# An FFT token mixer with a channel-mix behind it: the first transforms of later batches due 0.3 of a period sooner

## The chip, the cores and the metric

The kernel runs on one core of one Trainium2 chip. The metric is the device time of one execution in microseconds (us). Before the change the median was 607.15 us (three runs, 604.29 to 610.09).

TensorE (PE) multiplies, ScalarE (ACT) and VectorE (DVE) move results out of its accumulation banks and do the elementwise work, GpSimd (POOL) issues the loads of x, and SyncE (SP) issues nearly all other DMAs, one after the other in program order.

## The reference, cut to what matters

```python
# x: (8, 3072, 256) float32
X = np.fft.rfft(x, axis=1)
Yr = Xr @ w_r - Xi @ w_i + b_r
Yi = Xr @ w_i + Xi @ w_r + b_i
Y  = shrink(Yr, 0.01) + 1j * shrink(Yi, 0.01)     # sign(v) * max(|v| - 0.01, 0)
y  = np.fft.irfft(Y, n=3072, axis=1)              # tokens of the second half
xk = mu_k * y + (1 - mu_k) * y_prev;  xr = mu_r * y + (1 - mu_r) * y_prev
out = sigmoid(xr @ w_r2) * (relu(xk @ w_k) ** 2 @ w_v)
```

Each of the 8 batches passes through two transforms in two steps each (3072 = 96 x 32), and then through six token tiles of the channel-mix, which is the bulk of the matrix work.

## The kernel before

The transform of a batch of length 3072 is done as 96 x 32. Between the two steps of each transform the data change their layout by a "bounce": they are stored to device memory and read back differently. The stages of one batch are:

- `first`: first step of the forward transform (L279), 8 pairs of matmuls; results A are stored (L290, four stores of 384 KB), and when all four have landed they are read back as A2 (L304, eight reads of 192 KB). Each A store also sets off a load of x for the next batch (L68, from GpSimd).
- `middle`: second step, mixing with w_r and w_i, shrinking, first step back (L394, L422, L448); results V are stored in six groups of four 64 KB stores (L461) and read back (L472, four pieces of 384 KB): the second bounce.
- `last`: last step (L525), eight units; then the six token tiles (L611, L638, L655).

Below, "the boundary of batch b" (or boundary b) is the place where the last V stores of batch b, its read of V and its first L525 units stand.

```python
# in first(b): after the eviction of a group of A
def store(k):
    nc.sync.dma_start(out=Adr[b][:, 8 * q:8 * q + 8, :], in_=a)          # L290
    ...
        load_x(n // 4, n % 4)                                            # L68, next batch
    if q == 3:
        at(k + WRITE_US, fetch)
def fetch(k):
    for hf in range(2):
        A2[b, hf] = a2_pool.tile([128, NG // 2, D], BF16, name="A2")
        for cj in range(4):
            r0 = 24 * cj + 12 * hf
            nc.sync.dma_start(out=A2[b, hf][32 * cj:32 * cj + 32],       # L304
                              in_=Adr[b][r0:r0 + 12].rearrange("g n d -> n g d"))
...
# in middle(b): after the eviction of a group of V
def store(k):
    for cj in range(4):
        nc.sync.dma_start(out=Vdr[b][24 * cj + 4 * u:24 * cj + 4 * u + 4]...,
                          in_=vt[32 * cj:32 * cj + 32])                  # L461
    if u == NU - 1:
        at(k + (3.0 if b == 0 else WRITE_US), fetch)
def fetch(k):
    ...
    for q in (2, 3, 0, 1):
        nc.sync.dma_start(out=V2[b, q], in_=Vdr[b][:, 8 * q:8 * q + 8, :])   # L472
...
# order of the last step: the first unit needs pieces 2 and 3, the second pieces 0 and 1
order = ((1, 3), (0, 3), (0, 0), (0, 1), (0, 2), (1, 0), (1, 1), (1, 2))
```

A small planner in the kernel decides, while the program is built, in which order these units are put out. Each unit has a due time and a list of what it needs; among the units that its own clock calls ready, the one with the earliest due time is next. Engines execute in that fixed order. So a due time is not a time on the chip: it moves instructions, and with them the DMAs that hang on them, to another place in each engine's program.

```python
P = 71.5          # the planner's period, one batch
...
else:
    fb += first(b, s - 0.9 * P, s - 0.2 * P)
    fa += middle(b, s, s + 0.5 * P)
    fc += last(b, s + 0.75 * P, s + 0.95 * P)
```

## Time and profile before

| | before |
|---|---|
| median time | 607.15 us |
| span of the profiled run | 604.4 us |
| TensorE busy / VectorE / ScalarE | 94% / 86% / 72% |
| mean granted TensorE clock | 0.993 |
| waits of L525 for the read of V (PE and weight loads) | 12.8 us in 14 waits |

How to read this: TensorE is full, so its order is the time axis, and what costs time is only what makes it wait. The page's slices, the stretches of one period, TensorE's own timeline and the chain are shown in the prediction. The point to take from them is that in steady state nearly every period has 1 us of idle TensorE, and one has 4.

SyncE's own timeline around that place, at the boundary of batch 3 (start, duration of the issues together, operation, tensors, count):

```profile
241.86 1.88 SPq L461 DMA_DIRECT2D Vdr<-V  x4
244.44 0.68 SPq L290 DMA_DIRECT2D Adr<-A  x1
250.91 2.00 SPq L472 DMA_DIRECT2D V<-Vdr  x4
```

The read of V follows the last V stores with one A store between them. The reads of A come later, at 262.74.

### The profile page before, as it was taken

The numbers are of one execution on the slowest core, as the hardware profiler recorded it, in microseconds if no ns is written. First come the engines' busy times: TensorE is split into PE (matmuls) and PEld (weight loads), VectorE is DVE, ScalarE is ACT, GpSimd is POOL, SyncE is SP. The second block draws the span as 40 slices with busy tenths as digits, with TensorE's granted clock in tenths as the row PEclk, the third lists the DMA queues.
The fourth block names the chain that finished last, engine by engine and source line by source line (L and its number), as shares of the span: only waits on it lengthen the run. The fifth ranks groups of instructions, "written<-read, shape, count | busy, mean of one in ns | idle before, by whom it ended". The sixth has DMA issues, their size and how long they took to land.

```text
span 604.4 us, 12322 instructions
## 1 busy us (share of the span) xinstructions
PE 570.7 (94%) x4823; PEld 430.9 (71%) x4891; DVE 517.6 (86%) x839; ACT 436.3 (72%) x477; POOL 23.9 (4%) x53
## 2 busy tenths in 40 slices
PE   4977999999999999889999999999999999999996
PEld 3856766677767787667776777677776778776775
DVE  7677998789998899958988888979988889989983
ACT  6956986767776777567786768777787777667553
POOL 7001000000000000000000000000000000000000
PEclk9999999999999999989999999999999999999999
DMA  8945849864589555793569935785347834362224
GB/s 149 158 87 129 171 96 240 190 129 106 107 202 213 142 123 119 173 222 99 124 133 225 203 77 117 159 247 125 94 104 186 185 96 89 80 183 50 65 64 102
DMA packets 68878, 84.06 MB, mean 139 GB/s; under 512 B 9042, under 2 KB 53844, under 8 KB 68820
## 3 DMA queue, kind: packets, MB, share of 16 engines
q1 hardware_dynamic: 62916, 68.98, 45.8%
q0 software_dynamic: 5712, 14.03, 14.9%
q8 instruction: 38, 0.62, 0.4%
q10 hardware_dynamic: 192, 0.26, 0.2%
q14 instruction: 20, 0.16, 0.1%
HBM read 50.07 MB, written 47.19 MB: 161 GB/s over the span
## 4 chain that ended last, share of the span: by engine, by line
PE 80%; DMA 7%; DVE 5%; ACT 5%; issue 2%; SPq 1%; POOL 0%; ACTq 0%; POOLq 0%; DVEq 0%
PE banks L655 25%; PE banks L611 24%; PE banks L422 12%; PE banks L638 6%; DMA V<-Vdr 4%; PE banks L448 3%; PE banks L394 3%; PE banks L279 3%; PE banks L525 3%; ACT rl L617 2%; DMA Vdr<-V 2%; DMA xs<-in_x_dram 1%; ACT YT L226 1%; PE banks L352 1%; DVE Y L438 1%
## 5 line engine op out<-in xcount | busy, mean ns | idle before, releaser
L617 ACT ACTIVATE rl<-banks 128x1024 bf16<-128x1024 f32 x192 | 195.5, 1033 | 76.2 <-PE banks L611 75.2
L611 PE MATMUL banks<-xk,wk 128*128 128x512 bf16 x700 | 190.6, 379 | 5.3 <-ACT A L226 0.8
L655 PE MATMUL banks<-wv,k 128*128 128x256 bf16 x1536 | 183.4, 272 | 0.3 <-DVE k L623 0.3
L655 PEld LDWEIGHTS <-k 128*128 128x128 bf16 x1536 | 149.7, 98 | 30.3 <-issue 1.2
L623 DVE TENSOR_TENSOR k<-rl 128x1024 bf16<-128x1024 bf16 x192 | 131.1, 686 | 17.9 <-ACT rl L617 17.2
L611 PEld LDWEIGHTS <-wk 128*128 128x128 bf16 x768 | 73.0, 98 | 59.7 <-issue 3.5
L422 PEld LDWEIGHTS <-XT 128*128 128x128 bf16 x768 | 74.1, 98 | 17.2 <-issue 1.2
L422 PE MATMUL banks<-wr,XT 128*128 128x256 bf16 x384 | 73.3, 272 | 0.5 <-ACT YT L226 0.2
L422 PE MATMUL banks<-wi,XT 128*128 128x256 bf16 x384 | 73.3, 273 | 0.4 <-DVE XT L404 0.4
L589 DVE SCALAR_TENSOR_TENSOR xk<-diff,muk,YT 128x512 bf16<-128x512 bf16 x96 | 70.0, 745 | 0.5
L589 DVE SCALAR_TENSOR_TENSOR xr<-diff,mur,YT 128x512 bf16<-128x512 bf16 x96 | 68.9, 745 | 0.0
L666 DVE TENSOR_TENSOR o<-banks,rg 128x1024 f32<-128x1024 f32 (+1 forms) x49 | 58.7, 1197 | 5.8 <-PE banks L655 5.8
L226 ACT ACTIVATE YT<-banks 128x768 bf16<-128x768 f32 x60 | 46.4, 815 | 21.7 <-PE banks L525 19.0
L226 ACT ACTIVATE XT<-banks 128x1024 bf16<-128x1024 f32 (+2 forms) x46 | 44.9, 982 | 14.5 <-PE banks L394 14.3
L226 ACT ACTIVATE z<-banks 128x1024 bf16<-128x1024 f32 x38 | 38.9, 1024 | 22.0 <-PE banks L422 21.9
L638 PE MATMUL banks<-wrm,xr 128*128 128x256 bf16 x384 | 50.2, 274 | 1.7 <-ACT rl L617 1.5
L226 ACT ACTIVATE A<-banks 96x1024 bf16<-96x1024 f32 (+1 forms) x44 | 44.6, 1015 | 8.8 <-PE banks L279 6.7
L643 ACT ACTIVATE rg<-banks 128x1024 bf16<-128x1024 f32 x48 | 49.5, 1032 | 0.5 <-PE banks L638 0.5
L638 PEld LDWEIGHTS <-xr 128*128 128x128 bf16 x384 | 37.3, 98 | 12.4 <-issue 2.3
L226 ACT ACTIVATE V<-banks 128x1024 bf16<-128x1024 f32 x35 | 36.0, 1029 | 13.8 <-PE banks L448 9.8
L436 DVE TENSOR_TENSOR z<-z,bias 128x1024 bf16<-128x1024 bf16 x48 | 32.9, 686 | 9.5 <-ACT z L226 9.4
L525 PEld LDWEIGHTS <-V 96*128 96x128 bf16 x512 | 27.2, 98 | 13.5 <-DMA V<-Vdr 7.3
(100 smaller groups left out, 448.9 us busy)
## 6 DMA issues: line engine op xcount, KB each, us to landing
out_dram<-o SPq DMA_DIRECT2D x188, 128.0 KB, 2.3
xs<-in_x_dram POOLq DMA_DIRECT2D x32, 384.0 KB, 5.8
Vdr<-V SPq DMA_DIRECT2D x192, 64.0 KB, 1.8
V<-Vdr SPq DMA_DIRECT2D x32, 384.0 KB, 6.6
Adr<-A SPq DMA_DIRECT2D x24, 384.0 KB, 5.3
A<-Adr SPq DMA_DIRECT2D x48, 192.0 KB, 5.6
wk<-in_moe_w_k_dram POOLq DMA_DIRECT2D x1, 512.0 KB, 12.5
wv<-in_moe_w_v_dram POOLq DMA_DIRECT2D x1, 512.0 KB, 13.8
```

Source lines behind the costliest of these rows:

```text
L226: nc.scalar.activation(out, in_, AF.Copy, bias=0.0, scale=1.0)
L422: nc.tensor.matmul(o, lhs, w[:, c, :], start=(w is wr and c == 0), stop=(w is wi and c == NCD - 1))
L436: nc.vector.tensor_tensor(out=z, in0=z, in1=bias0 if u == 0 else bias, op=ALU.add)
L525: nc.tensor.matmul(pv[:, c, :, i, :], V2[b, n2 // 8][:, n2 % 8, 128 * c:128 * c + 128], FI, start=True, stop=True)
L589: nc.vector.scalar_tensor_tensor(out=m[:, c, :], in0=df[:, c, :], scalar=mu[:, c:c + 1], in1=yp[:, c, :], op0=ALU.mult, op1=ALU.add)
L611: nc.tensor.matmul(ps[:, 512 * f:512 * f + 512], wk[:, c, 128 * ff:128 * ff + 128], xk[:, c, :], start=(c == 0), stop=(c == NCD - 1))
L617: nc.scalar.activation(rl, ps, AF.Relu, bias=0.0, scale=1.0)
L623: nc.vector.tensor_tensor(out=k2, in0=rl, in1=rl, op=ALU.mult)
L638: nc.tensor.matmul(ps[:, 256 * q:256 * q + 256], xr[:, c, 128 * q:128 * q + 128], wrm[:, c, :], start=(c == 0), stop=(c == NCD - 1))
L643: nc.scalar.activation(rg, ps, AF.Sigmoid, bias=0.0, scale=1.0)
L655: nc.tensor.matmul(ps[:, 256 * q:256 * q + 256], K2[t][:, ff, 128 * q:128 * q + 128], wv[:, ff, :], start=(ff == 0), stop=(ff == NCF - 1))
L666: nc.vector.tensor_tensor(out=o[:, lo:hi], in0=ps[:, lo:hi], in1=rg[:, lo:hi], op=ALU.mult)
```

## The change

The intent, in the words that came with it: the first transforms of later batches are due 0.3 of a period sooner, so that their stores and the loads behind them end ahead of the second bounce's read.

```diff
-            fb += first(b, s - 0.9 * P, s - 0.2 * P)
+            fb += first(b, s - 1.2 * P, s - 0.5 * P)
```

## The prediction

> **What bounds the kernel now.** I read the page's totals and slices first, then busy time in stretches of one period each, then the waits, and the timeline only where they pointed.
>
> ```profile
> span 604.4 us, 12322 instructions
> PE 570.7 (94%) x4823; PEld 430.9 (71%) x4891; DVE 517.6 (86%) x839; ACT 436.3 (72%) x477; POOL 23.9 (4%) x53
> ...
> PE   4977999999999999889999999999999999999996
> ...
> PEclk9999999999999999989999999999999999999999
> ```
>
> TensorE is at nine tenths or more from slice 5 to the last but one. In stretches of 71.5 us (PE, PEld, DVE, ACT and POOL busy, granted clock, DMA share, GB/s):
>
> ```profile
> 120.00:191.50 71.50, 70.56 (x595) 53.25 (x602) 64.02 (x100) 53.10 (x58) 2.02 (x4) 1.00 0.65 148
> 191.50:263.00 71.50, 67.50 (x548) 50.23 (x556) 62.43 (x98) 49.38 (x53) 2.02 (x4) 0.98 0.68 155
> 263.00:334.50 71.50, 70.42 (x588) 52.81 (x596) 61.53 (x97) 54.77 (x61) 2.02 (x4) 1.00 0.69 155
> ```
>
> A normal period has 1.0 us of TensorE idle; one has 4.0 us and a lower clock. TensorE's timeline there (start, duration, idle before in brackets):
>
> ```profile
> 252.76 1.91 PE L655 MATMUL banks<-wv,k 128*128 128x256 bf16 x16
> 256.72 0.34 PE L525 MATMUL banks<-FI,V 96*128 96x96 f16 x4 [2.05 <-DMA V<-Vdr]
> 257.94 0.34 PE L525 MATMUL banks<-FI,V 96*128 96x96 f16 x4 [0.87 <-DMA V<-Vdr]
> 258.12 0.41 PE L611 MATMUL banks<-xk,wk 128*128 128x512 bf16 x1
> 258.75 1.06 PE L611 MATMUL banks<-xk,wk 128*128 128x512 bf16 x2 [0.22 <-issue]
> 259.60 0.53 PE L525 MATMUL banks<-FI,V 96*128 96x96 f16 x4
> 260.56 0.50 PE L525 MATMUL banks<-FI,V 96*128 96x96 f16 x4 [0.43 <-DMA V<-Vdr]
> ```
>
> The last transforms of batch 3 (L525) wait for the second bounce's read: 2.05 + 0.87 + 0.22 + 0.43 = 3.6 us. The chain shows why:
>
> ```profile
> 243.28 7.49 DMA Vdr<-V
> ...
> 252.21 8.30 DMA V<-Vdr
> ```
>
> The batch's last V store, 1.8 us in the median, took 7.5 us beside an x load issued at 243.65 and an A store at 244.44, so the read began only at 250.91. This is the collision that the change is after. It is the only large one: the other readings of V cost TensorE at most 0.3 us each in steady periods. The whole prize is thus about 4 us in 604.
>
> **What the Trainium skill says.** "DMA: Bandwidth & Descriptors", section "Issuing engines are not separate DMA queues": DMAs of all issuing engines run on the same 16 DMA engines and interleave. The trace agrees: the quiet read of V for batch 7 took 7.9 us from first issue (530.25) to last landing (531.59 + 6.59), the one of batch 3, with an x load issued at 250.60 beside it, 9.65 us. The same page, "Queues, rings and completion order": an engine consumes one row's descriptors in ring order. The trace agrees: output stores issued behind the A reads at 194.49 landed after 5.9 to 6.3 us, against 2.3 us in the median. The same page, "Anatomy of one DMA": any semaphore wait happens on the issuing sequencer, before dispatch. Here that is SyncE, in program order. "TensorE: Matmul & The Clock Gate", section "What's actually happening": an idle window of about 3.4 us halves the clock. Here the granted clock was 0.73 over 256 to 261 us and 0.81 over 261 to 263: by my arithmetic (0.27 x 5 + 0.19 x 2) x 2 = 3.5 us at half speed after a stall of 3.6 us.
>
> **The change part by part.** Nothing is added or removed: TensorE has 9784 rows before and after, and its busy 570.7 us stay. What moves is the place of 48 pairs of L279 matmuls and what hangs on them: A stores, reads of A (8 of 192 KB a batch), x loads. I take places from the built program's instruction order and count TensorE time between them with this trace's durations (16 of L655 1.75 us, 4 of L611 0.86, 8 of L638 0.88, 2 of L279 0.43, 4 of L448 0.43, 8 of L525 0.34), because TensorE is full.
>
> Before, SyncE's order around a boundary is: last V stores, A store, read of V, outputs, A store, read of A. After, for batches 2 to 6 (five boundaries), it is: last A store of the next batch, four V stores, four output stores, *eight reads of A*, the last four V stores, read of V. The A reads have moved from behind the second bounce's read to straight in front of it. This is the step on which I bet.
>
> TensorE's clock, zero at the last L279 pair: to the last L448 of the batch 0.43 + 0.43 + 1.75 + 0.86 + 0.88 + 0.86 = 5.2 us. From there to the first L525: 0.43 + 0.86 + 1.75 + 0.86 + 1.75 + 0.86 + 0.88 + 1.73 + three L279 pairs 1.29 + 1.75 + 0.86 + 1.75 = 14.8, so the first L525 unit is due at 20.0, the second at 20.0 + 0.34 + 0.86 = 21.2. (Before, this distance was 14.8 to 15.7 too, just enough.)
>
> The DMA chain on the same clock. A's eviction queues behind one other on ScalarE: store issued at about 2.4. It lands 4.2 to 6.1 us later in this trace when an x load is near, say 5: 7.4. The fourth output store takes the semaphore of the DMA eight issues earlier, this A store, and waits for it; the A reads start at T = 7.7. Their cost from this trace (issue duration, issue times, landing min/median/max):
>
> ```profile
> L304 SPq DMA_DIRECT2D A<-Adr x8: 322/468/469, 190.5 to 193.9; - x8
> ...
> DMA to landing us min/median/max: 3.0/5.5/6.5
> ```
>
> The eighth is issued at 193.9 and lands 6.5 later: 9.9 us after T. The last V stores stand behind them in the ring, and the first four also wait for the A reads eight issues back. Four small stores at 0.3 us each (my estimate from the spacing of the outputs that follow such reads): landed at T + 11.1, and the read of V is issued at T + 11.2. Quiet, that read gives:
>
> ```profile
> L472 SPq DMA_DIRECT2D V<-Vdr x4: 314/376/377, 530.2 to 531.6; - x4
> ...
> DMA to landing us min/median/max: 3.9/5.6/6.6
> ```
>
> Second piece at about +5.3, fourth at +7.9, that is 24.2 and 26.8. The first unit needs pieces 1 and 2: stall 24.2 - 20.0 = 4.2. The second, now due at 25.4, needs 3 and 4: 1.4 more. Together 5.6 us a boundary, five times: 28.
>
> The x load of the batch after next is released by the second of the three L279 pairs, at 15.3 + 0.4 on this clock, in the middle of the tail of this chain. There are such loads at three of the five boundaries (x ends with batch 7). Its cost by the skill's sharing and the two reads above is 9.65 - 7.9 = 1.7: together 5. After each stall TensorE runs some 3.4 us at half speed, partly still idle; around 260 us it cost 0.8 (8 of L638 1.48 instead of 1.04, two L525 groups 0.53 and 0.50 instead of 0.34); with longer stalls I say 1.0 each: 5. Given back: batch 3's 3.6 + 0.8 = 4.4.
>
> Sum: 604.4 + 28 + 5 + 5 - 4.4 = 638 us of span. The profiled run's time was 1.8 us above its span (606.18 against 604.4): 640.
>
> **Rivals.** (a) The intent holds: A data land before the last V store needs the ring, the 4 us come back and nothing is added: 602 to 603, within 2%. For it: the A stores and x loads do leave the read's neighbourhood in part. Against it: the order in the ring, which no timing can change. Even with the A store landing in 3.0 us, the best in the trace, T is about 5.7 and 3.6 us of stall a boundary remain: 5 x 3.6 - 4.4 = +14, 620. (b) Worse: an x load starves small V stores, as the 7.49 us store did, 5.7 more than usual; at three boundaries that is +17, about 657. For it: the x load again starts as V stores are queued. Against: it could be paid inside the A reads' time. (c) Another engine takes over: the earlier pairs shift evictions between ScalarE and VectorE (ScalarE's rows 381 to 367, VectorE's 774 to 775), and SyncE's blocking delays outputs whose two buffers VectorE needs. VectorE is at 62 to 64 of 71.5 us a period, and a stalled TensorE gives it room; under 3 us.
>
> **Range and chances.** The five boundaries repeat one order, so an error in T or in the read times counts five times: 2 us there is 10 us. Low end 619, the best case of (a); high end 656, near (b). Slower by over 2% is above 619: 0.9. Within 2% needs the stall under 3.5 us a boundary: 0.07. Faster by 2% would need more than the idle time that exists in steady state: 0.03.
>
> **What would show it.** Right: the waits of L525 for V grow from about 13 us over PE and PEld together to tens; five gaps of 4 to 10 us on TensorE, 70 to 80 us apart, before L525; the granted clock drops in five slices; periods of about 77 us; SyncE's last V stores issued after the A reads and landing late; TensorE's busy time unchanged but for the slow clock. Wrong: read of V issued less than 8 us after the last L448, or gaps at other lines (L279 for x, L394 for A).

## The result, and the profile after

The changed kernel took 645.0 us in the median (four runs, 642.29 to 648.13) against 606.58 of the kernel before (four runs with the earlier three). The ratio is 1.063, 95% interval 1.0559 to 1.0701. Ratios here and below are the mean time of one kernel's fast runs over that of the other's fast runs of the same rounds, so they are not quite the ratios of the medians. The prediction was 640, range 619 to 656, slower with a chance of 0.9. The profiled run of the changed kernel was the slowest of the four (648.13 us, mean clock 0.955 against 0.965 to 0.968), so the profile shows somewhat more slow clock than the median run has.

The page's lines after, answering to those in the prediction:

```profile
span 646.2 us, 12403 instructions
PE 596.2 (92%) x4891; PEld 442.9 (69%) x4891; DVE 521.5 (81%) x843; ACT 437.2 (68%) x473; POOL 23.7 (4%) x53
...
PE   4979898999996999889997999979999799999997
PEclk9997999999997999979999799988999799999999
```

The slices show a dip of TensorE and of its clock every fourth or fifth slice of 16.2 us, which is once per period. (TensorE's busy time isn't comparable by itself: 68 of the matmul records of the trace before are missing, and slow matmuls count as busy.)

Two of the stretches of 71.5 us, in the columns of the prediction:

```profile
191.50:263.00 71.50, 65.90 (x543) 49.14 (x542) 57.17 (x92) 46.97 (x50) 1.52 (x3) 0.95 0.53 134
263.00:334.50 71.50, 65.95 (x535) 48.55 (x534) 56.20 (x90) 48.93 (x53) 2.02 (x4) 0.95 0.58 134
```

TensorE now idles 5.6 us in each, at a lower clock, where it idled 1 us before in an ordinary period. SyncE's timeline at the same boundary of batch 3:

```profile
258.23 1.79 SPq L677 DMA_DIRECT2D out_dram<-o  x4
260.11 5.10 SPq L304 DMA_DIRECT2D A<-Adr  x8
265.31 2.19 SPq L461 DMA_DIRECT2D Vdr<-V  x4
271.86 1.88 SPq L472 DMA_DIRECT2D V<-Vdr  x4
```

The eight reads of A now stand in front of the last V stores. The V stores were issued over 265.31 to 267.5 and the read of V could start only at 271.86, 11.75 us after the first read of A. TensorE's timeline there (start, duration, idle before in brackets):

```profile
270.29 1.91 PE L655 MATMUL banks<-wv,k 128*128 128x256 bf16 x16
276.28 0.34 PE L525 MATMUL banks<-FI,V 96*128 96x96 f16 x4 [4.08 <-DMA V<-Vdr]
277.72 0.50 PE L525 MATMUL banks<-FI,V 96*128 96x96 f16 x4 [1.10 <-DMA V<-Vdr]
278.02 1.91 PE L611 MATMUL banks<-xk,wk 128*128 128x512 bf16 x4
...
280.62 0.50 PE L525 MATMUL banks<-FI,V 96*128 96x96 f16 x4 [0.37 <-DMA V<-Vdr]
280.92 1.91 PE L638 MATMUL banks<-wrm,xr 128*128 128x256 bf16 x8
```

TensorE waits 4.08 + 1.10 + 0.37 = 5.55 us, and then L611 and L638 take 1.91 us each where they took 1.03 and 1.04: the clock is halved. The clock column (seventh: 0.50) in two stretches after such waits, at batches 3 and 5:

```profile
277.51:284.34 6.83, 6.25 (x42) 3.99 (x43) 1.83 (x8) 4.12 (x5) 0.00 (x0) 0.50 0.78 285
431.11:441.35 10.24, 8.38 (x51) 4.91 (x52) 2.60 (x8) 4.37 (x5) 0.00 (x0) 0.50 0.73 224
```

The same picture stands at all five boundaries, batches 2 to 6: waits of 5.6, 5.55, 5.4, 4.0 and 3.3 us, 23.8 in all. The waits of L525 for V over TensorE and its weight loads, first before, then after (us, times):

```profile
  DMA V<-Vdr: 12.8, 14
```

```profile
  DMA V<-Vdr: 60.5, 41
```

Where the time went: the span grew by 646.2 - 604.4 = 41.8 us. The five waits are 23.8. A sixth, at the boundary of batch 1, is 2.8 (0.70 + 1.31 + 0.75) and was not there before. The old wait at batch 3 (3.6) is replaced. That makes 23.8 + 2.8 - 3.6 = 23.0 of idle TensorE; the other 18.8 is what is left over, and by the clock record most of it is work at a slow clock. (Between the medians the growth is 38.4, not 41.8.) Over the five boundaries 33.3 us of TensorE's busy time lie in half-speed stretches; if all of it ran at half speed, that is a loss of up to 16.7.

### The profile page after: what moved, and what is told of

Same layout as the page of the kernel before. It is cut to its first block, busy times and chain, and to the rows that moved or that the text cites. A ratio compares the mean times of both kernels' runs of the same rounds, so it can differ in the third digit from the quotient of the medians.

```text
span 646.2 us, 12403 instructions
## 1 busy us (share of the span) xinstructions
PE 596.2 (92%) x4891; PEld 442.9 (69%) x4891; DVE 521.5 (81%) x843; ACT 437.2 (68%) x473; POOL 23.7 (4%) x53
## 4 chain that ended last, share of the span: by engine, by line
PE 79%; DMA 9%; DVE 4%; ACT 4%; SPq 2%; issue 1%; POOL 1%; POOLq 0%; ACTq 0%; DVEq 0%
PE banks L655 24%; PE banks L611 23%; PE banks L422 12%; DMA V<-Vdr 7%; PE banks L638 6%; PE banks L525 3%; PE banks L448 3%; PE banks L279 3%; PE banks L394 3%; PE banks L352 1%; DMA Vdr<-V 1%; ACT rl L617 1%; SPq L461 1%; ACT V L226 1%; DMA A<-Adr 1%
## 5 line engine op out<-in xcount | busy, mean ns | idle before, releaser
L611 PE MATMUL banks<-xk,wk 128*128 128x512 bf16 x768 | 200.6, 389 | 0.6 <-ACT rl L617 0.4
L611 PEld LDWEIGHTS <-wk 128*128 128x128 bf16 x768 | 75.0, 100 | 58.5 <-issue 5.6
L226 ACT ACTIVATE YT<-banks 128x768 bf16<-128x768 f32 x55 | 42.3, 814 | 45.7 <-PE banks L525 43.4
L525 PE MATMUL banks<-FI,V 96*128 96x96 f16 x512 | 37.6, 227 | 27.0 <-DMA V<-Vdr 26.6
L525 PEld LDWEIGHTS <-V 96*128 96x128 bf16 x512 | 31.4, 109 | 39.6 <-DMA V<-Vdr 33.9
L226 ACT ACTIVATE z<-banks 128x1024 bf16<-128x1024 f32 x42 | 43.0, 1024 | 19.3 <-PE banks L422 19.1
L638 PE MATMUL banks<-wrm,xr 128*128 128x256 bf16 x384 | 54.1, 288 | 0.0
L226 ACT ACTIVATE XT<-banks 128x1024 bf16<-128x1024 f32 (+2 forms) x44 | 43.2, 985 | 12.9 <-PE banks L394 12.2
L638 PEld LDWEIGHTS <-xr 128*128 128x128 bf16 x384 | 39.1, 103 | 12.2
L226 ACT ACTIVATE V<-banks 128x1024 bf16<-128x1024 f32 x33 | 34.0, 1030 | 11.3 <-PE banks L448 7.6
```

Of the source, the lines that this page charges most:

```text
L226: nc.scalar.activation(out, in_, AF.Copy, bias=0.0, scale=1.0)
L525: nc.tensor.matmul(pv[:, c, :, i, :], V2[b, n2 // 8][:, n2 % 8, 128 * c:128 * c + 128], FI, start=True, stop=True)
L611: nc.tensor.matmul(ps[:, 512 * f:512 * f + 512], wk[:, c, 128 * ff:128 * ff + 128], xk[:, c, :], start=(c == 0), stop=(c == NCD - 1))
L638: nc.tensor.matmul(ps[:, 256 * q:256 * q + 256], xr[:, c, 128 * q:128 * q + 128], wrm[:, c, :], start=(c == 0), stop=(c == NCD - 1))
```

## The experiments

The theory: the reads of A, 1.5 MB, stand in SyncE's order in front of the last V stores, so the read of V comes late and L525 waits. Rival 1: it is what else moved, an x load and an A store that now fall into the read of V. Rival 2: the planner shifted evictions between ScalarE and VectorE. The runs share a chip and the runs of the kernel before: e1 to e4 (608.02 us before), e5 to e8 (607.65), e9 to e11 (605.28). All results were correct.

### e1: only the A reads held back

```diff
                 def fetch(k):
+                    if b >= 3 and ("V2", b - 1) not in done:
+                        at(k + 0.3, fetch)
+                        return
                     for hf in range(2):
```

> The changed kernel with one thing undone: the eight reads of A of the next batch are issued after the read of V of this batch instead of in front of its last V stores (batches 2 to 6). All matmul pairs, A stores and x loads stay early. Theory (the A reads stand in front of the last V stores in the ring): the gaps before L525 at boundaries 2 to 6 (23.7 us together) and the half-speed clock behind them vanish; time 599 to 608 us. Rival 1 (the moved L279 pairs bring an x load and an A store into the read of V): the gaps stay, 630 us or more. Rival 2 (evictions shifted between ScalarE and VectorE): as rival 1, time stays near 640.

Measured: 606.73 us, ratio 0.9968 (0.9946 to 0.9989). SyncE's timeline at batch 3:

```profile
251.53 2.72 SPq L464 DMA_DIRECT2D Vdr<-V  x4
255.72 1.72 SPq L475 DMA_DIRECT2D V<-Vdr  x4
257.49 9.95 SPq L307 DMA_DIRECT2D A<-Adr  x8
```

The read of V starts 255.72 - 251.53 = 4.2 us after the first of its V stores is issued (6.55 us in the changed kernel), and those stores come straight after the outputs. No wait for V over 0.25 us is left at boundaries 2 to 6. The whole loss is gone while all matmul pairs, A stores and x loads stay early. Rivals 1 and 2 fall as the main cause. The place of the reads is it.

### e2: the kernel before, with eight such reads added

```diff
                 def store(k):
+                    if u == NU - 1 and 2 <= b <= 6:
+                        for hf in range(2):
+                            for cj in range(4):
+                                r0 = 24 * cj + 12 * hf
+                                nc.sync.dma_start(out=A2[b, hf][32 * cj:32 * cj + 32],
+                                                  in_=Vdr[b - 1][r0:r0 + 12].rearrange("g n d -> n g d"))
                     for cj in range(4):
```

> The kernel before with one thing added: eight reads of the same shape and size as the reads of A (from an older V buffer in memory into an A tile that is no longer used) in front of the last V stores of batches 2 to 6. No matmul pair moves. Theory: the read of V is issued some 11 us after the first of these and TensorE waits 4 to 7 us at each of five boundaries, with a slow clock behind: 630 to 655 us. Rivals 1 and 2 (it is the moved pairs): no move, so 604 to 615 us, the extra 7.5 MB being hidden.

Measured: 646.99 us, ratio 1.0638 (1.0604 to 1.0671), a loss as large as that of the change, with no unit moved. That the size is the same is partly chance: its waits for V at the five boundaries add up to 30.3 us, against 23.8 in the changed kernel. SyncE at batch 3, then TensorE:

```profile
251.85 5.95 SPq L464 DMA_DIRECT2D A<-Vdr  x8
257.90 3.27 SPq L467 DMA_DIRECT2D Vdr<-V  x4
262.14 0.32 SPq L290 DMA_DIRECT2D Adr<-A  x1
267.24 1.72 SPq L478 DMA_DIRECT2D V<-Vdr  x4
```

```profile
271.19 0.50 PE L531 MATMUL banks<-FI,V 96*128 96x96 f16 x4 [6.53 <-DMA V<-Vdr]
```

So the reads are sufficient too. The kernel e2 moves 7.5 MB more than the others, but e1 moves the bytes of the changed kernel in another order, and loses nothing.

### e3 and e4: less shift, more shift

```diff
-            fb += first(b, s - 1.2 * P, s - 0.5 * P)
+            fb += first(b, s - 1.1 * P, s - 0.4 * P)      # e3
+            fb += first(b, s - 1.3 * P, s - 0.6 * P)      # e4
```

> A third of the shift: due from s - 1.1 P (before 0.9, changed 1.2). In the built order the A reads then stand directly behind the read of V. Theory: no stall, and the x load and A store of batch 3's collision have moved too: 599 to 608 us. Rival (earlier pairs cost in proportion, whatever the ring's order): between the two kernels, 625 to 635 us.

> A third more shift: due from s - 1.3 P. The A reads then stand in front of the last two groups of V stores, and by the built order start 7 us earlier against the last V eviction, so they end at about the time when that eviction is done. Theory: V stores land 5 to 6 us after the last L448 starts, the fourth piece of V at about 14, due at 16: no or hardly any stall, 600 to 612 us. Rival (cost grows with the shift): over 650 us.

Measured: e3 611.57 us, ratio 1.0053 (1.0027 to 1.008); e4 623.42 us, ratio 1.022 (1.0171 to 1.0269, its one slow run of four left out). The cost is not in proportion to the shift: 1.1 costs 0.5%, 1.2 costs 6.3%, 1.3 costs 2.2%. Both missed their ranges on the slow side, though. In e3 the waits for V at boundaries 3 to 6 are 1.0 to 1.45 us: an A store still stands right in front of the read of V, and A reads right behind it. Three new waits of 0.7 to 1.0 us at L394, for VectorE, come on top. No run took these causes apart. In e4 waits of 2 to 4.6 us stay at boundaries 2 to 4. GpSimd's timeline of e4 shows two x loads right after the read of V was issued at 334.63, and TensorE's shows what followed:

```profile
335.47 0.51 POOL L68 DMA_DIRECT2D xs<-in_x_dram  x1 [22.59 <-PE banks L279]
336.34 0.51 POOL L68 DMA_DIRECT2D xs<-in_x_dram  x1 [0.35 <-PE banks L279]
```

```profile
345.96 1.08 PE L525 MATMUL banks<-FI,V 96*128 96x96 f16 x12 [2.55 <-DMA V<-Vdr]
```

From first issue to last piece this read took 11.3 us, against 7.9 for the quiet one. This points to rival 1 in e4, and e6 tests it.

### e6: e4 with those two x loads held

```diff
# cut: store calls load at its own time in place of load_x, and the due factor is 1.3
+                def load(k):
+                    n = 4 * b + q + 4
+                    if b >= 4 and q < 2:
+                        if ("V2", b - 2) not in done:
+                            at(k + 0.3, load)
+                            return
+                        nc.gpsimd.tensor_copy(out=n1c[0:96], in_=V2[b - 2, 1][:, 0, 0:1])
+                    load_x(n // 4, n % 4)
+                    done["x", n // 4, n % 4] = k + 18.0
```

> The due factor 1.3 again (623 us, waits for V of 2 to 4.6 us at three boundaries), with the two x loads that ran beside the read of V held back until that read has landed (a one-column copy on GpSimd reads V first). Theory: the remaining waits there are the x loads' sharing of the DMA engines, so the waits at boundaries 2, 3 and 4 vanish: 604 to 612 us. Rival (the A reads in front of two V store groups still delay the chain): 618 us or more.

Measured: 612.55 us, ratio 1.0078 (1.0025 to 1.0131), half a microsecond above the range. The waits for V at boundaries 2 to 4 fell from 2.2 to 4.6 us to 0.5 to 1.3. So x loads do matter where two of them meet the read. The size is not clean: the loads' new planner times also moved batch 1's last step later.

### e8: the same order on SyncE, but the last step due later

```diff
-            fc += last(b, s + 0.75 * P, s + 0.95 * P)
+            fc += last(b, s + (0.92 if b >= 2 else 0.75) * P, s + (1.04 if b >= 2 else 0.95) * P)
```

> The changed kernel with SyncE's order as it is (A reads in front of the last V stores), but the last transforms of batches 2 to 7 are due 0.17 P later: in the built order the first L525 unit stands 3.5 us later and the second 7.8 us later. Theory (the loss is landing of V against the place of L525): the wait shrinks to under 2 us a boundary and the clock mostly stays full: 606 to 622 us. Rival (the A reads' order hurts elsewhere, outputs or evictions): stays above 630. If the mixing of the next tokens begins to starve, gaps will show at L611 instead.

Measured: 618.31 us, ratio 1.018 (1.0135 to 1.0224). The waits at the five boundaries are 1.57, 1.29, 0.95, under 0.25 and 2.0 us. Late data cost what TensorE's order leaves uncovered; giving the order 3.5 to 7.8 us of slack brought the ratio from 1.063 down to 1.018, without touching a DMA.

### e5, e9 and e10: the slow clock and the x load

```diff
# e5: in front of the first and the second L525 unit
+                for _ in range(({0: 12, 1: 5}.get(n, 0)) if 2 <= b <= 6 else 0):
+                    nc.tensor.matmul(ps[:, 0:512], wr[:, 0, 0:128], bias[:, 0:512], start=True, stop=True)
# e9: the x load that starts in the tail of the A reads waits for V
+                        if b >= 4 and q == 0:
+                            nc.gpsimd.tensor_copy(out=n1c[0:96], in_=V2[b - 2, 1][:, 0, 0:1])
                         load_x(n // 4, n % 4)
# e10: both
```

> The changed kernel with 12 idle matmuls (128x512 on constant data, overwritten in place) in front of the first and 5 in front of the second L525 unit of batches 2 to 6: 3.7 us of work per boundary inside a wait that measured 3.3 to 5.6 us. The data of V arrive no sooner. Theory (part of the loss is the halved clock after each wait, not the wait): half-speed time of 41 us at the five boundaries mostly goes, and the time falls from 645 to 625 to 635 us although more work is done. Rival (the clock record costs nothing, the read alone sets the time): 643 to 650 us.

> The changed kernel with the one x load that starts in the tail of the A reads (first group of the batch after next, boundaries 2 to 4) held until the read of V has landed. It measures the prediction's x term (1.7 us at three boundaries, 5 us) and its rival b (17 us). Prediction's term right: 3 to 7 us faster than the changed kernel, 638 to 642 us. Rival b: 628 us or less. No effect: 644 to 647 us.

> e9 with the idle matmuls of e5 (12 and 5 at five boundaries). In e5 an x load reached a V store at boundary 3 and delayed V itself, which confuses the reading; here it can't. If the slow clock after the waits costs what its records say (33.3 us of TensorE busy time at half speed at the five boundaries, so up to 16.7 us of loss): 622 to 632 us, 8 to 17 us less than e9. Prediction's term (1.0 us each): 5 us less than e9. Rival (no cost): equal to e9.

Measured: e5 641.29 us, ratio 1.0545 (1.0491 to 1.0598); e9 643.81, 1.0638 (1.06 to 1.0676); e10 634.63, 1.0479 (1.0443 to 1.0514).

The run e5 is confounded. The half-speed time at the five boundaries fell from 41 to 10 us, but at boundary 3 an x load was issued at 268.97, ahead of the last V store at 269.21, and that store landed 6.7 us later (in the changed kernel the store came first and took 4.5). The read of V thus started at 276.06, 2.6 us after TensorE's last useful matmul had ended there, instead of 0.3 us before it. The wait itself had grown.

In e9 that x load cannot be there. It shows the prediction's x term: 1.0638 is the changed kernel's loss again, so holding the load gained nothing that these rounds resolve. The first two pieces of V arrived 0.8 us sooner after issue (3.57 and 4.66 us against 4.37 and 5.40), the last did not.

The run e10 against e9 shows the clock: 0.0159 of 605 us, 9.6 us less, with the data no sooner and 3.7 us more TensorE work per boundary. A stretch behind the waits of boundary 3, e9 first, then e10 (the clock is the seventh column):

```profile
273.00:279.80 6.80, 5.46 (x37) 3.48 (x37) 1.71 (x8) 3.90 (x5) 1.19 (x3) 0.52 1.02 296
```

```profile
269.00:275.00 6.00, 4.53 (x46) 2.91 (x47) 1.64 (x7) 3.29 (x4) 1.24 (x3) 1.00 1.03 333
```

All half-speed stretches at the boundaries are gone (mean clock 0.993). So the slow clock costs about 10 us of the change's loss. This is a net figure: where the idle matmuls ran on after the data had come, they cost time of their own. It is the smaller part: with a full clock the kernel is still 4.8% slower.

### e11: the A reads on another queue

```diff
-                            nc.sync.dma_start(out=A2[b, hf][32 * cj:32 * cj + 32],
+                            (nc.gpsimd if b >= 3 else nc.sync).dma_start(out=A2[b, hf][32 * cj:32 * cj + 32],
```

> The changed kernel with the reads of A of batches 3 to 7 issued by GpSimd, at the same time but on its own queue, so that SyncE's V stores and the read of V stand behind none of them in program order or ring; the 16 DMA engines are shared as before. Theory (order in one queue is what costs): waits for V of 0 to 3 us a boundary, 608 to 628 us. Rival (the same bytes at the same time on the same engines cost the same in any queue): 636 to 650 us.

Measured: 632.89 us, ratio 1.0463 (1.0415 to 1.0511). That is outside the theory's range and outside the rival's. The last V stores at boundary 3, now behind nothing in SyncE's queue (issue durations and times, landing min/median/max):

```profile
L461 SPq DMA_DIRECT2D Vdr<-V x4: 322/446/473, 256.8 to 258.2; - x4
...
DMA to landing us min/median/max: 5.4/7.6/7.8
```

The first of them was issued 1.2 us after the first A read (255.63) instead of 5.2 us after it, but they took up to 7.8 us to land, against 1.8 in the median of the kernel before. The read of V was issued at 266.10, 10.5 us after the first A read, against 11.75 in the changed kernel. An x load of GpSimd ran there as well (260.51). But at boundaries 5 and 6, which have no x load, the read of V still came 9.0 and 9.8 us after the first A read (11.7 and 11.4 in the changed kernel). So leaving the queue recovers a quarter of the loss: most of the delay stays when the reads are only in flight at the same time, and the smaller part goes when they no longer stand in front of the stores in one queue. The Trainium skill, "DMA: Bandwidth & Descriptors", section "Queues, rings and completion order", says that each DMA engine takes packets of the queues that have work in turn. The run agrees that a queue of one's own is no way past: the small stores wait either way.

### e7: a version that beats both

e1 left a wait of 2.65 us for V at batch 1, beside early x loads and A stores of batch 2. So e7 is e1 with batch 2's old due:

```diff
-            fb += first(b, s - 1.2 * P, s - 0.5 * P)
+            a0 = 0.9 if b == 2 else 1.2
+            fb += first(b, s - a0 * P, s - (a0 - 0.7) * P)
```

> The kernel of e1 (early pairs, A reads held behind the read of V), but batch 2 keeps its old due of 0.9 P, because in e1 TensorE waited 2.65 us for V of batch 1 with early x loads beside its read. Theory: that wait goes, 602 to 605 us, ratio 0.990 to 0.995 to the kernel before. Rival: the gain of e1 was all there is: 0.997 or more.

Measured: 600.88 us (six runs, 600.31 to 602.69), ratio 0.9892 (0.9856 to 0.9927). That is 1.1% faster than the kernel before, and slightly better than expected. The stretch that holds the old collision:

```profile
191.50:263.00 71.50, 71.03 (x599) 53.31 (x597) 63.92 (x101) 53.24 (x57) 2.02 (x4) 1.00 0.69 154
```

TensorE idles 0.5 us there instead of 4.0. The intent of the change was sound, once the A reads are kept out of the way.

## Why the prediction was right

**The bound and the prize.** TensorE's order as time axis held, and a prize of about 4 us was the right size: with the damage taken out, the change is worth 0.3% or 1.9 us (e1), and 1.1% or 6.6 us with batch 2 left alone (e7).

**The step of the bet**, that the A reads move in front of the last V stores, held and is the cause: undone alone it gives everything back (e1), done alone it costs 6.4% (e2). One reason given for it was too narrow. It said that the stores stand behind the reads in the ring; e11 shows that most of the delay stays when they don't, while the same engines are busy with the reads.

**The chain of times.** On the prediction's clock (zero at the last L279 pair, 251.88 us in the trace after) against the trace at batch 3:

| step | predicted | measured |
|---|---|---|
| first A read issued (T) | 7.7 | 260.11: 8.2 |
| read of V issued | T + 11.2 = 18.9 | 271.86: 20.0 |
| first L525 unit due | 20.0 | 272.20: 20.3 |
| second piece of V there | 24.2 | 277.72: 25.8 |
| fourth piece there | 26.8 | 280.62: 28.7 |
| wait at the boundary | 5.6, and 1.7 for x | 5.55 |

**The sum.** It came out 5 us short of the median, with terms that were off both ways, so that it came as close as it did is partly luck.

| term | predicted | measured |
|---|---|---|
| waits at five boundaries | 28 | 23.8 |
| x load at three of them | 5 | nothing resolved (e9) |
| slow clock after the waits | 5 | about 10 (e10); at most 16.7 by the record |
| batch 1 and the start | none | 2.8 of wait, and slow clock behind it |

The waits were smaller because the last pieces of V arrived under work that the slow clock had stretched: L611 took 1.91 us between the second and the fourth piece, not the 0.86 of the prediction. The x term was worked out from a read of V with an x load beside it from its start (e4 and e6 show that such loads do cost); here the load met the A reads' tail. The clock was taken from one 3.5 us stretch before, while the five boundaries had 41 us of half speed. That stretch was also read a little wrong: it did not follow a stall of 3.6 us, but began at 258.34, after the first two waits (2.05 and 0.87 us) and before the others. The wait at batch 1 was not looked for at all. There the first L525 unit came 7.1 us sooner (105.29 against 112.40), while the read of V was issued 4.2 us later (98.94 against 94.72), among moved A stores and x loads. Against e1, e7 regained 0.76% of the time by leaving batch 2 alone, some 4.6 us.

**The rivals.** (a), the intent: 602 to 603, lies between what e1 and e7 reach, but only with the reads held. (b), the starved V store, did not decide the time of the changed kernel, but e5 caught it once, at boundary 3. (c), another engine: nothing; the built order of e1 on ScalarE and VectorE is that of the changed kernel up to batch 7, and e1 is not slower than before.

**What stays open.** How much of the span that neither waits nor e10 explain (18.8 us less about 10) is slow clock at the boundaries that e10's matmuls merely covered, slow clock at batch 1 and the start, or differences between single profiles, was not separated. Only the start can be set aside: its 10.24 us at half speed (3.41 in the kernel before) do not come from the change, since e2 and e7, with the old order there, have 10.24 too, and e1 and e9, with the new one, have 3.41.

## What to carry to other kernels

A due time or a priority moves whole bundles of DMAs, so before shipping such a change list what each DMA queue issues between the producer of the latency-critical transfer and its consumer, in the built order; the question is what comes in front of it, more than how early the rest ends. Keep bulk reads that nobody waits for behind the short store-and-read pair that someone does, by order, since another queue gave back only a quarter of the loss here. When a full TensorE begins to wait, count the slow clock behind the wait too: here it was about 10 us beside 24 us of waits.

## What the Trainium skill lacked or had wrong

- "TensorE: Matmul & The Clock Gate", section "Why this matters for your kernels", advises no idle gaps of over about 3 us between bursts. Here shorter gaps were enough: at batch 5 the clock fell at 431.11, 2.2 us into a gap of 2.40 us, and at batch 1 it fell at 110.26 after gaps of 0.70, 1.31 and 0.75 us. The page does speak elsewhere of frequent short idle times with this effect; what it lacks is a length for them.
- The same page, section "What's actually happening", describes a free-running window of 3.413 us. The trace of the changed kernel agrees: the half-speed stretches at the five boundaries begin at 199.00, 277.51, 352.60, 431.11 and 509.62, which are 23, 22, 23 and 23 such steps apart, and each lasts two or three steps (6.83 or 10.24 us), 41 us in all. What the page lacks is how much of a window must be idle. Here the steps just before these five falls had 2.06 to 3.07 us of idle TensorE and the one before the fall at 110.26 had 1.87, while one with 1.90 (270.69 to 274.10) was followed by no fall. The last step of each of the five stretches had at most 0.25 us. So small waits inside a slow stretch prolong it by whole steps.
- "DMA: Bandwidth & Descriptors", section "Queues, rings and completion order", describes the turns between queues but gives no figure for a small store beside bulk reads of another queue. Here 64 KB stores landed after 5.4 to 7.8 us with eight 192 KB reads and an x load in flight on GpSimd's queue, and after 3.8 to 7.0 us with the reads alone (e11, boundaries 3, 5 and 6), against 1.8 us in the median of the kernel before.
- No page has the cost of bulk reads put between a store and its read-back: eight reads of 192 KB in front of the last stores delayed the issue of the read-back to 11.75 us after the first of them.
